# Attention scores masked by VectorE instead of TensorE, with the softmax division and one block load moved earlier

## The chip, the cores and the metric

The kernel runs on one core of one Trainium2 chip. The metric is the device time of one launch, in microseconds (us), on that core. TensorE multiplies matrices, VectorE and ScalarE work element by element on what it leaves in PSUM, GpSimd does the same on SBUF, and SyncE issues the transfers. [...]

## The reference

Three layers in a row. An attention over windows (32 heads in all, 768 positions, chunks of 32 queries that see 16 keys to the left, 8 to the right, and 8 memory keys), a dense layer with a gated activation, and a mixture of eight experts whose gates are balanced by eight rounds of normalisation.

```python
scores = scale * np.matmul(q_c, k_full.transpose(0, 1, 3, 2))
scores = scores - np.max(scores, axis=-1, keepdims=True)
a = np.exp(scores)
a = a / (np.sum(a, axis=-1, keepdims=True) + 1e-09)
out[:, :, c_start:c_end] = np.matmul(a, v_full)
...
h = x @ w_in
g = h * np.clip(h + 3.0, 0.0, 6.0) / 6.0
x = (g @ w_out)
...
for e in range(E):
    out += P[:, e:e + 1] * (np.maximum(x @ w1[e], 0.0) @ w2[e])
```

## The kernel before, in words

The program has three stages: a first stretch that holds the attention and the dense layer (two passes over the hidden columns of that layer), a short one for the gates, and the experts. The change lies in the first stretch alone.

**Attention units.** The attention is cut into 32 units of 96 queries (three chunks) by 128 keys, all eight heads of one batch entry. The three chunks of a unit see different keys, so a mask (0 or a very large negative number) has to be added to the scores. `a_scores` does that on TensorE: for each half of four heads, one product of two short bf16 tables (`mask`, L266) writes the mask into a PSUM bank (`sc`), and the four products of queries and keys (L272) add to it. Then, for a unit: `a_max` takes the row maxima of both halves on VectorE (`mx`, L279) and `a_neg` scales them (`nm`, L285); `a_exp` takes the exponentials on ScalarE, one instruction per head with its row sum (`e<-sc`, L297); `a_norm` divides on VectorE (`sm`, `rc`, `e<-e,rc`, L305 to L308); `a_transpose` turns the eight blocks on TensorE (`pt`, L315) and copies them out on ScalarE (`et`, L167); `a_values` multiplies by the values (`av`, L335); and `a_split` writes the result as a high part (ScalarE, `xh`, L167), a low part (VectorE, `xl`, L353) and their sum for later use (GpSimd, L359).

**The dense layer** runs in steps, numbered `i`: one step is one block of rows and one slice of 128 hidden columns. A step has a first product (`layer_product`, `ph`), an activation (`layer_relu` on ScalarE, L405; `layer_times` on VectorE, L410), a split into parts (`hh` on ScalarE, L167; `hl` on VectorE, L427), and, two steps later, a second product (`second`, `pa`). Every product is three products of float parts (L229 to L231). The first pass has 64 steps with blocks of 384 rows, the second 48 with blocks of 512.

**What sets the order.** Units 0 to 13 and the first 16 steps are issued by a list of words (`OPENING`). From step 17 on, a loop issues one unit per two steps. The odd step has, in program order, the first product and its activation and split, then values and split of unit u, scores and maximum of unit u+2, the second product, the exponentials of u+2, and the division of u+1. The even step has its first product and activation, the second product, the transposes of the unit, and only then its split:

```python
            if due:
                stage(a_values, u)
                stage(a_split, u)
                stage(a_scores, u + 2)
                stage(a_max, u + 2)
                ...
            second(i - LAG)
            ...
            if due:
                stage(a_exp, u + 2)
                stage(a_load, u + 4)
                stage(a_norm, u + 1)
```

In the same loop ScalarE and VectorE still convert weights (L147, L149; L158, L160), GpSimd combines expert weights (L692), and at the end of each block the accumulators are emptied: the second block's by VectorE (L500) in step 17, the later ones by ScalarE (L505). In the last block of the first pass `x_load(0)` fetches the first block of rows for the second pass in step f = 1 and `x_split(0, r)` splits it in steps f = 3 to 6.

Of the kernel before, what the change touches and what calls it, by code (L numbers as in the profile page):

```python
# [9 lines left out]
F32 = mybir.dt.float32  # L10
# [3 lines left out]
AF = mybir.ActivationFunctionType  # L14
ALU = mybir.AluOpType
AX = mybir.AxisListType
PSUM = bass.MemoryType.PSUM

D = 64
NH = 8  # L20
UQ = 96
UK = 128
# [4 lines left out]
UPS = 8  # L27
# [6 lines left out]
B2 = 512  # L34
# [6 lines left out]
LEAD = 1  # L41
STEADY = 12
EARLY = (1, 2, 3, 4, 5, 6, 7, 8, 9)
OPENING = (
# [22 lines left out]
def attn_moe_moe(ctx: ExitStack, tc: tile.TileContext, qk, vw, wi, wo, wa, wb, wg, out):  # L67
    nc = tc.nc
# [16 lines left out]
    sm_p = ctx.enter_context(pool("sm", 2))  # L85
    dr_p = ctx.enter_context(tc.tile_pool(name="dr", bufs=1, space=bass.MemoryType.DRAM))
    one, two, three = (ExitStack() for _ in range(3))
    ps_a = one.enter_context(pool("ps_a", 4, PSUM))
# [142 lines left out]
        nc.tensor.matmul(ps, wl, xh, start=False, stop=stop, skip_group_check=more)  # L231


    qk_t, v_t, sc_t, e_t, pt_t, et_t, av_t = {}, {}, {}, {}, {}, {}, {}
    xs = {}
    mask = []

# [7 lines left out]
    def mask_load(_):  # L245
# [5 lines left out]
        nc.vector.tensor_copy(out=mask[0][:3], in_=t[:3])  # L251
        nc.vector.tensor_copy(out=mask[0][D:D + 3], in_=mask[0][:3])

    def v_load(u):
        t = at_p.tile([UK, NH * D], F32, tag="vw", name="vw", bufs=2)
        nc.sync.dma_start(out=t, in_=vw[u])
        v_t[u] = t

    def a_scores(u):

        t, ps, tag = qk_t.pop(u), *((ps_a, "a") if u in EARLY else (ps_s, "s"))
        seen = {0: 0, UPS - 1: 1}.get(u % UPS, 2)
        for j in range(2):
            sc_t[u, j] = ps.tile([UQ, 4, UK], F32, tag=tag, name="sc")
            m = mask[0][D * j:D * j + D]
            nc.tensor.matmul(  # L266
                sc_t[u, j], m[:, 0, :UQ], m[:, seen, UQ:].unsqueeze(1).to_broadcast([D, 4, UK]),
                start=True, stop=False, skip_group_check=True)
        for i in range(4):
            for j in range(2):  # L270
                k = t[D * j:D * j + D, i]
                nc.tensor.matmul(  # L272
                    sc_t[u, j][:, i], k[:, :UQ], k[:, UQ:], start=False, stop=i == 3, skip_group_check=True)

    def a_max(u, halves=(0, 1)):
        for j in halves:
            if j == 0:
                e_t[u] = sm_p.tile([UQ, NH], F32, tag="mx", name="mx")
            nc.vector.tensor_reduce(out=e_t[u][:, 4 * j:4 * j + 4], in_=sc_t[u, j], axis=AX.X, op=ALU.max)  # L279
        if len(halves) == 2:  # L280
            a_neg(u)

    def a_neg(u):
        nm = sm_p.tile([UQ, NH], F32, tag="nm", name="nm")
        nc.vector.tensor_scalar_mul(nm, e_t[u], -SCALE)  # L285
        e_t[u] = nm

    def a_exp(u, halves=(0, 1)):
        for j in halves:
            if j == 0:  # L290
                ef = at_p.tile([UQ, NH, UK], F32, tag="e", name="e", bufs=2)
                sm = sm_p.tile([UQ, NH], F32, tag="sm", name="sm")
                e_t[u] = e_t[u], ef, sm
            nm, ef, sm = e_t[u]
            sc = sc_t.pop((u, j))
            for h in range(4 * j, 4 * j + 4):
                nc.scalar.activation(  # L297
                    out=ef[:, h], in_=sc[:, h % 4], func=AF.Exp, scale=SCALE, bias=nm[:, h:h + 1],
                    accum_out=sm[:, h:h + 1])
        if 1 in halves:  # L300
            e_t[u] = ef, sm
# [68 lines left out]
    def x_tiles():  # L370
        return [x_p.tile([128, KT, B1], F32R, tag=f"x{t}", name=f"x{t}") for t in "hl"]
# [7 lines left out]
    def stage(do, u):  # L379
        if u < NU:  # L380
            do(u)
# [81 lines left out]

    def opening(do, i):
        acts = {
            "qk": a_load, "mk": mask_load, "sc": a_scores, "v": v_load, "raw": raw_load, "sp": spill_one, "xps": spill_x2, "wg": gate_weights,
            "no": idle, "nm": a_neg, "n": a_norm, "V": a_values, "xh": a_high, "xl": a_low, "xf": a_whole,
            "ca": single_act, "cv": single, "hi": single_hi, "lo": single_lo,
            "F": layer_product, "re": layer_relu, "t": layer_times, "hh": layer_high, "hl": layer_low}
        two = {"mx": a_max, "ex": a_exp}  # L470
        if do in acts:
            acts[do](i)
        elif do[0] == "D":
            {"hi": single_hi, "xh": a_high, "hh": layer_high,
             "eta": lambda u, e: a_copy(u, 0, e), "etb": lambda u, e: a_copy(u, 1, e)}[do[1:]](i, nc.vector)
        elif do[:2] in two:
            two[do[:2]](i, (0,) if do[2] == "a" else (1,))
        elif do[0] == "T":
            a_turn(i, "ab".index(do[1]))
        elif do[:2] == "et":  # L480
            a_copy(i, "ab".index(do[2]))
        elif do == "S":
            second(i, False)
        elif do == "ev":
            evacuate(*steps[i])
# [32 lines left out]
    xq = []  # L518

    def x_pieces():  # L520
        return [t.rearrange("p k n -> p (k n)").rearrange("p (k n) -> p k n", n=B2) for t in x_tiles()]

    def x_load(b):
        if b < 2:
            xq.extend(x_pieces() for _ in range(2 - b))
        for kt in range(KT):
            n, at = ((0, kt) if kt < 3 else (1, 0)) if b % 2 == 0 else ((2, kt) if kt < 3 else (1, 1))
            xs.setdefault((1, b), []).append([t[:, at] for t in xq[n]])
        u = b * B2 // UQ
        t = xl_p.tile([128, UPB, KT, UQ], F32, tag="xl", name="xl")  # L530
        spare = [v[:, 2, :KT * UQ].bitcast(F32).rearrange("p (k q) -> p k q", k=KT) for v in xq[1]]
        c = UPB - u % UPB
        nc.sync.dma_start(out=t[:, :c], in_=xd[u // UPB][:, UPB - c:])
        if c < UPB:
            nc.sync.dma_start(out=t[:, c:], in_=xd[u // UPB + 1][:, :UPB - c])
        for i in range(2):
            v = u + UPB + i
            nc.sync.dma_start(out=spare[i], in_=xd[v // UPB][:, v % UPB])
        parts = []
        for i in range(UPB + 2):  # L540
            a, e = (min(max(v - b * B2, 0), B2) for v in (UQ * (u + i), UQ * (u + i + 1)))
            o = a + b * B2 - UQ * (u + i)
            whole = i < UPB and e - a == UQ
            if whole and parts and parts[-1][0] == "whole":
                parts[-1] = "whole", parts[-1][1], e, parts[-1][3], i + 1
            elif whole:
                parts.append(("whole", a, e, i, i + 1))
            else:
                parts.append(("part", a, e, t[:, i] if i < UPB else spare[i - UPB], o))
        xf_t[b] = t, parts  # L550
# [116 lines left out]
    w1s, w1, w2s, w2, gq, op, yc = {}, {}, {}, {}, {}, {}, {}  # L667
# [466 lines left out]
    with tc.manual_schedule():  # L1134
        at_ctx = pool("at", 2, side="right")
        at_p = at_ctx.__enter__()
# [3 lines left out]
        make_identity(nc, ident)  # L1140
        for word in OPENING:
            opening(word.rstrip("0123456789"), int(word.lstrip("abcdefghijklmnopqrstuvwxyzABCDEFGHIJKLMNOPQRSTUVWXYZ")))
# [19 lines left out]
        for i, (pe, b, f) in enumerate(steps):  # L1162
            if i < 2 * NF:
                continue
            u, turn, due = (i - 2 * NF) // 2 + 3 * UPB, i % 2 == 0, i % 2 == 1
# [22 lines left out]
            sums_due(i)  # L1188
            if pe == 0 and b == NB1 - 1:
                w_load(f)  # L1190
                if f == 1:
                    x_load(0)
            if pe == 1 and f == 1 and b + 1 < NB2:
                x_load(b + 1)
# [7 lines left out]
            if due:  # L1202
                stage(a_values, u)
                stage(a_split, u)
                stage(a_scores, u + 2)
                stage(a_max, u + 2)
                convert_act(rate(i))
                stage(v_load, u + 2)
# [8 lines left out]
            if due:  # L1217
                stage(a_exp, u + 2)
                stage(a_load, u + 4)
                stage(a_norm, u + 1)  # L1220
            if pe == 0 and not due:
                if turn:
                    stage(a_transpose, u)
# [7 lines left out]
                w_split(NF - LAG + f)  # L1231

            n = b + 1 if pe else 0
            r = f - 3
            if 0 <= r < KT and n < NB2 and (pe or b == NB1 - 1):
                x_split(n, r)
            if (pe, b, f) == (1, 2, 6):
# [44 lines left out]
        at = {o: i for i, (_, o) in enumerate(order)}  # L1282
        makes = {}
        for n in range(NM):
            for mi in range(7):
                for r in range(4):
                    i = at[n, mi - 1, r] if mi else at[n, 0, 0] - 4 + r
# [3 lines left out]
        halves, fours, quarter_work = {}, {}, None  # L1291
        sums = {}
        for sb in range(1, NSB):
# [5 lines left out]
            for r in range(2, 12):  # L1299
                i = base + (r + (r - 2) // 2 if sb == 1 else r + 7 if r > 2 else 8)  # L1300
# [11 lines left out]
        for i, (h, o) in enumerate(order):  # L1312
# [26 lines left out]
            if h and h[1] in FORM:  # L1339
                deep_out(*h, 0)  # L1340
                while lows:
                    do, n = lows.pop(0)
# [5 lines left out]
            while lows:  # L1348
                do, n = lows.pop(0)
# [9 lines left out]
            if h and h[1] in FORM:  # L1359
                n, _, p = h  # L1360
# [12 lines left out]
            elif h:  # L1373
                n, k, p = h
# [19 lines left out]
            if i in fours:  # L1394
                rows = []
                for q in range(2):
                    t = out_p.tile([128, HB], F32, tag="o", name="xs", bufs=NO)
# [71 lines left out]
```

## Time and profile before

| | before |
|---|---|
| median of 3 runs (lowest, highest) | 2497.66 us (2496.04, 2498.72) |
| profiled execution: its own time | 2497.8 us |
| its span, first to last instruction | 2496.0 us |
| TensorE busy | 2483.2 us (99%) |
| VectorE, ScalarE, GpSimd busy | 1967.8, 1443.9, 951.4 us |
| granted TensorE clock | 1.000 |

A busy share is the time in which an engine has an instruction in flight. In a timeline row stand start, length, engine, line, operation, output and inputs, the number of instructions joined in the row, and in brackets how long the engine stood idle before it and what it waited for. A start-to-start distance says more than a length here, since an instruction's end overlaps the next one's start.

### The profile page before, as it was taken

To read this page: it belongs to the slowest core of one execution; us is meant where nothing else is said; L and a number is where in the kernel's file an instruction comes from. 1 tells how busy PE (TensorE), PEld (TensorE's weight loads), DVE (VectorE), ACT (ScalarE), POOL (GpSimd) and SP (SyncE) were. 2 spreads that over 40 slices of the span, in tenths; PEclk is the share of its full clock that TensorE was granted. 3 is DMA by queue.
4 is the path that set the end of the run, shared out by engine and by line. 5 is a ranking of instruction groups with operands and counts; after the bars stand their busy time and mean duration, and the time that the engine had idled before them with its cause. 6 is when DMAs were issued, how large, how long until landed. Compare 5 with 4: busy or idle time off the path is not lost. (4 is left out here: it accounts for less than half of the span.)

```text
span 2496.0 us, 37061 instructions
## 1 busy us (share of the span) xinstructions
PE 2483.2 (99%) x13125; PEld 2123.1 (85%) x13125; DVE 1967.8 (79%) x2422; ACT 1443.9 (58%) x2685; POOL 951.4 (38%) x705
## 2 busy tenths in 40 slices
PE   9999999999999999999999999999999999999999
PEld 8999998787778888888888888888888888888888
DVE  8867656576689999999986778777888678777777
ACT  8666653222365565556666665656666666655665
POOL 0155656665025554533443324333323233132321
PEclk9999999999999999999999999999999999999999
DMA  7689988877466766766667777666777667676664
GB/s 210 188 279 312 302 271 294 292 269 256 135 214 208 228 214 229 226 221 226 232 233 253 262 257 246 221 214 232 251 267 237 223 223 229 227 231 213 213 220 155
DMA packets 379990, 587.45 MB, mean 235 GB/s; under 512 B 30675, under 2 KB 229276, under 8 KB 379804
## 3 DMA queue, kind: packets, MB, share of 16 engines
q1 hardware_dynamic: 379520, 584.85, 72.0%
q8 instruction: 103, 1.69, 0.3%
q14 instruction: 83, 0.68, 0.1%
q10 hardware_dynamic: 284, 0.24, 0.0%
HBM read 444.36 MB, written 140.61 MB: 234 GB/s over the span
## 5 line engine op out<-in xcount | busy, mean ns | idle before, releaser
L986 POOL TENSOR_TENSOR g<-g,pb 128x512 f32<-128x512 f32 x304 | 564.9, 1876 | 1181.4 <-ACT g L979 849.4
L1037 ACT ACTIVATE oh<-g 128x1024 fp32r<-128x1024 f32 x336 | 355.1, 1057 | 357.8 <-PE oa L231 107.2
L1042 DVE TENSOR_TENSOR ol<-g,oh 128x1024 fp32r<-128x1024 f32 x336 | 456.2, 1359 | 56.4 <-ACT oh L1037 56.1
L692 POOL TENSOR_TENSOR fr<-fr 128x256 f32<-128x256 f32 x320 | 278.1, 870 | 180.0 <-DMA fr<-in_wa_dram 88.2
L229 PE MATMUL ga<-xo,w1h 128*128 128x512 f32 (+1 forms) x864 | 314.1, 364 | 2.1 <-ACT g L954 1.5
L230 PE MATMUL ga<-xo,w1h 128*128 128x512 f32 (+1 forms) x864 | 312.5, 362 | 0.0
L231 PE MATMUL ga<-xo,w1l 128*128 128x512 f32 (+1 forms) x864 | 312.5, 362 | 0.0
L1012 DVE TENSOR_TENSOR g<-g 128x1024 f32<-128x1024 f32 x192 | 302.0, 1611 | 0.0
L230 PE MATMUL oa<-ol,w2h 128*128 128x512 f32 x760 | 298.0, 392 | 0.0
L229 PE MATMUL oa<-oh,w2h 128*128 128x512 f32 x760 | 297.5, 391 | 0.0
L231 PE MATMUL oa<-oh,w2l 128*128 128x512 f32 x760 | 296.1, 390 | 0.0
L859 ACT ACTIVATE w1h<-w1s 128x512 fp32r<-128x512 f32 (+1 forms) x416 | 249.9, 601 | 39.3 <-issue 19.0
L971 DVE TENSOR_TENSOR g<-g,ga 128x512 f32<-128x512 f32 x192 | 130.4, 679 | 103.7 <-PE ga L231 103.5
L405 ACT ACTIVATE t<-ph,half 128x384 f32<-128x384 f32 (+1 forms) x112 | 70.5, 630 | 242.1 <-PE ph L231 236.9
L979 ACT ACTIVATE g<-g 128x512 f32<-128x512 f32 x288 | 178.0, 619 | 40.5 <-DVE g L971 40.3
L229 PE MATMUL gc<-xo,w1h 128*128 128x512 f32 (+1 forms) x544 | 195.6, 359 | 1.6 <-ACT g L954 0.8
L896 ACT ACTIVATE w2h<-w2s 128x1024 fp32r<-128x1024 f32 x168 | 176.9, 1053 | 32.0 <-DMA w2s<-in_wb_dram 21.2
L231 PE MATMUL gc<-xo,w1l 128*128 128x512 f32 (+1 forms) x544 | 194.7, 358 | 0.0
L230 PE MATMUL gc<-xo,w1h 128*128 128x512 f32 (+1 forms) x544 | 194.6, 358 | 0.0
L229 PEld LDWEIGHTS ga<-xo,w1h 128*128 128x128 f32 x864 | 162.6, 188 | 35.4 <-ACT g L954 3.4
L230 PEld LDWEIGHTS ga<-xo,w1h 128*128 128x128 f32 x864 | 162.6, 188 | 28.5
L231 PEld LDWEIGHTS ga<-xo,w1l 128*128 128x128 f32 x864 | 162.5, 188 | 25.0
(188 smaller groups left out, 5657.6 us busy)
## 6 DMA issues: line engine op xcount, KB each, us to landing
w1l<-wl SPq DMA_DIRECT2D x232, 256.0 KB, 4.2
w2l<-wl SPq DMA_DIRECT2D x112, 512.0 KB, 3.8
w1s<-ws SPq DMA_DIRECT2D x192, 256.0 KB, 4.9
w2s<-ws SPq DMA_DIRECT2D x96, 512.0 KB, 4.9
ws<-fr SPq DMA_DIRECT2D x80, 512.0 KB, 5.0
w2s<-in_wb_dram SPq DMA_DIRECT2D x144, 256.0 KB, 3.6
wl<-w1l SPq DMA_DIRECT2D x128, 256.0 KB, 4.0
wl<-w2l SPq DMA_DIRECT2D x56, 512.0 KB, 4.4
```

The costliest lines, as they stand in the source:

```text
L229: nc.tensor.matmul(ps, wh, xh, start=start, stop=False, skip_group_check=more)
L230: nc.tensor.matmul(ps, wh, xl, start=False, stop=False, skip_group_check=more)
L231: nc.tensor.matmul(ps, wl, xh, start=False, stop=stop, skip_group_check=more)
L692: nc.gpsimd.tensor_tensor(out=o, in0=a, in1=b, op=f)
L859: nc.scalar.activation(out=w1_part(g, w1[g]), in_=w1_part(g, w1s[g]), func=AF.Copy)
L896: nc.scalar.activation(out=hi, in_=w2s[m], func=AF.Copy)
L971: nc.vector.tensor_tensor(out=g, in0=g, in1=ps, op=ALU.add)
L979: nc.scalar.activation(out=g, in_=g, func=AF.Relu)
L986: nc.gpsimd.tensor_tensor(out=g, in0=g, in1=p, op=ALU.mult)
L1012: nc.vector.tensor_tensor(out=o, in0=gq[n, x, i], in1=gq[n, y, i], op=ALU.subtract)
L1037: nc.scalar.activation(out=hi, in_=gq[n, b, i], func=AF.Copy)
L1042: nc.vector.tensor_tensor(out=lo, in0=gq[n, b, i], in1=op[m, i].bitcast(F32), op=ALU.subtract)
```

## The change

- From unit 14 on (all units of the loop) the mask is no longer a product. Ahead of the first unit, `mask_make` forms the three masks in PSUM by three small products and ScalarE copies them once into SBUF (`mk`). `a_max` then adds the mask to each half of the scores on VectorE, writing to the SBUF tile `e`, takes the maxima of all eight heads by one reduction of that tile, and `a_exp` reads `e` instead of PSUM.
- In the odd step the division of unit u+1 stands right behind the split of unit u, ahead of scores and maximum of u+2. Before, it stood at the end of the step.
- `x_load(0)` is issued in step f = 0 of the last block instead of f = 1, `x_split(0, r)` in f = 2 to 5 instead of 3 to 6, and the two pieces of memory that the block uses change places.

```diff
+ADDED = 14
 OPENING = (
-    "mk0 qk0 no12 sc0 mxa0 raw3 ...
+    "mk0 qk0 no12 mm0 sc0 mxa0 raw3 ...
...
+    def mask_make(_):
+        m = mask[0][:D]
+        ps = ps_a.tile([UQ, 3, UK], F32, tag="a", name="sc")
+        for k in range(3):
+            nc.tensor.matmul(ps[:, k], m[:, 0, :UQ], m[:, k, UQ:], start=k == 0, stop=k == 2, skip_group_check=True)
+        t = sm_p.tile([128, B2], F32, tag="lt", name="mk", bufs=1)[:UQ, :3 * UK]
+        mask.append(t.rearrange("p (k n) -> p k n", k=3))
+        nc.scalar.activation(out=mask[1], in_=ps, func=AF.Copy)
...
     def a_scores(u):
...
-            nc.tensor.matmul(
-                sc_t[u, j], m[:, 0, :UQ], m[:, seen, UQ:].unsqueeze(1).to_broadcast([D, 4, UK]),
-                start=True, stop=False, skip_group_check=True)
+            if u < ADDED:
+                nc.tensor.matmul(
+                    sc_t[u, j], m[:, 0, :UQ], m[:, kind(u), UQ:].unsqueeze(1).to_broadcast([D, 4, UK]),
+                    start=True, stop=False, skip_group_check=True)
...
     def a_max(u, halves=(0, 1)):
         for j in halves:
             if j == 0:
                 e_t[u] = sm_p.tile([UQ, NH], F32, tag="mx", name="mx")
-            nc.vector.tensor_reduce(out=e_t[u][:, 4 * j:4 * j + 4], in_=sc_t[u, j], axis=AX.X, op=ALU.max)
+                if u >= ADDED:
+                    ef_t[u] = at_p.tile([UQ, NH, UK], F32, tag="e", name="e", bufs=2)
+            if u >= ADDED:
+                nc.vector.tensor_tensor(
+                    out=ef_t[u][:, 4 * j:4 * j + 4], in0=sc_t.pop((u, j)),
+                    in1=mask[1][:, kind(u)].unsqueeze(1).to_broadcast([UQ, 4, UK]), op=ALU.add)
...
         if len(halves) == 2:
+            if u >= ADDED:
+                nc.vector.tensor_reduce(out=e_t[u], in_=ef_t[u], axis=AX.X, op=ALU.max)
             a_neg(u)
...
     def a_exp(u, halves=(0, 1)):
...
-            sc = sc_t.pop((u, j))
+            sc = ef[:, 4 * j:4 * j + 4] if u >= ADDED else sc_t.pop((u, j))
...
-            xq.extend(x_pieces() for _ in range(2 - b))
+            xq.extend([x_pieces() for _ in range(2 - b)][::-1])
...
-                if f == 1:
+                if f == 0:
                     x_load(0)
...
                 stage(a_split, u)
+                stage(a_norm, u + 1)
                 stage(a_scores, u + 2)
...
                 stage(a_load, u + 4)
-                stage(a_norm, u + 1)
...
-            r = f - 3
+            r = f - 2 - pe
```

How the instructions of one unit stand on VectorE in the middle of the loop, before (`hl` and `t` belong to the dense layer, `sa` and `sb` to the conversion of weights, the rest is named above):

```order
L427 TENSOR_TENSOR hl<-t,hh 128x384
L353 TENSOR_TENSOR xl<-av,xh 128x4x96
L279 TENSOR_REDUCE mx<-sc 96x4 x2
L285 TENSOR_SCALAR nm<-mx 96x8
L305 TENSOR_SCALAR sm<-sm 96x8
L307 RECIPROCAL rc<-sm 96x8
L308 TENSOR_TENSOR e<-e,rc 96x1024
L158 SCALAR_TENSOR_TENSOR sa<-raw,rest 128x512
L160 SCALAR_TENSOR_TENSOR sa<-pw,sa 128x512
L410 SCALAR_TENSOR_TENSOR t<-t,ph 128x384
```

And the same unit on VectorE in the changed kernel:

```order
L452 TENSOR_TENSOR hl<-t,hh 128x384
L378 TENSOR_TENSOR xl<-av,xh 128x4x96
L330 TENSOR_SCALAR sm<-sm 96x8
L332 RECIPROCAL rc<-sm 96x8
L333 TENSOR_TENSOR e<-e,rc 96x1024
L297 TENSOR_TENSOR e<-sc,mk 96x512 x2
L305 TENSOR_REDUCE mx<-e 96x8
L310 TENSOR_SCALAR nm<-mx 96x8
L159 SCALAR_TENSOR_TENSOR sa<-raw,rest 128x512
L161 SCALAR_TENSOR_TENSOR sa<-pw,sa 128x512
L435 SCALAR_TENSOR_TENSOR t<-t,ph 128x384
```

Between `xl` and `nm` there stood two instructions before; now there stand six, the three of the division among them.

ScalarE in the changed kernel, over the same stretch of the loop (L430 is the activation of a step, L168 the copies `et`, `hh` and `xh`, L322 the exponentials):

```order
L322 ACTIVATE e,sm<-e,nm 96x128 x8
L430 ACTIVATE t<-ph,half 128x384
L168 ACTIVATE et<-pt 128x384 x2
L168 ACTIVATE hh<-t 128x384
L430 ACTIVATE t<-ph,half 128x384
L168 ACTIVATE hh<-t 128x384
L168 ACTIVATE xh<-av 128x4x96
L148 ACTIVATE rest<-raw 128x512
```

Here nothing moved; only the exponentials read `e` where they read `sc` before. The copies `et`, which the values product of the next unit needs, stand behind the eight exponentials.

## Rows read from the trace of the kernel before

**Rows 1.** Windows, loop and after: length; PE, PEld, DVE, ACT, POOL busy; clock, DMA.

```profile
137.00:332.00 195.00, 194.76 (x1554) 184.40 (x1556) 132.84 (x222) 128.45 (x441) 113.56 (x125) 1.00 0.99 307
300.00:660.00 360.00, 360.00 (x1819) 304.85 (x1818) 225.14 (x365) 113.02 (x285) 198.08 (x228) 1.00 0.78 258
```

**Rows 2.** Timeline of PE, one unit of the loop.

```profile
162.71 0.88 PE L335 MATMUL av<-et,vw 128*64 128x96 f32 x16
163.52 0.42 PE L266 MATMUL sc<-mask 64*96 64x512 bf16 x2
163.77 1.04 PE L272 MATMUL sc<-qk 64*96 64x128 f32 x16
...
173.98 0.88 PE L335 MATMUL av<-et,vw 128*64 128x96 f32 x16
```

**Rows 3.** Timeline of ACT, the same unit.

```profile
162.88 0.58 ACT L405 ACTIVATE t<-ph,half 128x384 f32<-128x384 f32 x1 [1.23 <-PE ph L231]
164.07 0.52 ACT L167 ACTIVATE hh<-t 128x384 fp32r<-128x384 f32 x1 [0.62 <-DVE t L410]
164.50 0.47 ACT L167 ACTIVATE xh<-av 128x384 fp32r<-128x384 f32 x1
...
167.14 0.36 ACT L297 ACTIVATE e<-sc,nm 96x128 f32<-96x128 f32 x1 [1.06 <-DVE sm L305]
...
169.90 0.60 ACT L405 ACTIVATE t<-ph,half 128x384 f32<-128x384 f32 x1
171.64 0.87 ACT L167 ACTIVATE et<-pt 128x384 f32<-128x384 f32 x2 [1.15 <-PE pt L315]
172.40 0.53 ACT L167 ACTIVATE hh<-t 128x384 fp32r<-128x384 f32 x1
```

**Rows 4.** Timeline of DVE, the same unit.

```profile
164.63 0.56 DVE L427 TENSOR_TENSOR hl<-t,hh 128x384 fp32r<-128x384 f32 x1 [0.59 <-ACT hh L167]
165.10 0.55 DVE L353 TENSOR_TENSOR xl<-av,xh 128x384 fp32r<-128x384 f32 x1
165.57 1.27 DVE L279 TENSOR_REDUCE mx<-sc 96x4 f32<-96x512 f32 x2
166.88 0.17 DVE L285 TENSOR_SCALAR nm<-mx 96x8 f32<-96x8 f32 x1
166.96 0.16 DVE L305 TENSOR_SCALAR sm<-sm 96x8 f32<-96x8 f32 x1
...
168.53 1.23 DVE L158 SCALAR_TENSOR_TENSOR sa<-raw,rest 128x512 uint32<-128x512 uint32 x1
```

**Rows 5.** Groups by form, 137 to 332 us: count, busy, mean ns, idle before.

```profile
L427 DVE TENSOR_TENSOR hl<-t,hh 128x384 fp32r<-128x384 f32 x35 | 25.6, 730 | 33.6 <-ACT hh L167 33.6
L279 DVE TENSOR_REDUCE mx<-sc 96x4 f32<-96x512 f32 x34 | 21.6, 676 | 0.0
L285 DVE TENSOR_SCALAR nm<-mx 96x8 f32<-96x8 f32 x17 | 5.3, 309 | 0.6
L167 ACT ACTIVATE hh<-t 128x384 fp32r<-128x384 f32 x35 | 18.4, 525 | 10.9 <-DVE t L410 10.9
L167 ACT ACTIVATE et<-pt 128x384 f32<-128x384 f32 x36 | 15.7, 489 | 14.7 <-PE pt L315 14.7
```

**Rows 6.** One line, a reduction out of SBUF: ns least, median, most.

```profile
L605 DVE TENSOR_REDUCE rs<-Pm x8: 352/353/354, 660.4 to 692.0; 128x24 f32<-128x192 f32 x8
```

**Rows 7.** Timelines of DVE and PE around step 17.

```profile
130.80 0.54 DVE L353 TENSOR_TENSOR xl<-av,xh 128x384 fp32r<-128x384 f32 x1
133.07 1.93 DVE L500 TENSOR_TENSOR x<-x,pa 128x384 f32<-128x384 f32 x4
134.19 0.33 PE L229 MATMUL pa<-hh,wbh 128*128 128x384 f32 x1
137.24 0.85 PE L315 MATMUL pt<-ident,e 96*128 96x96 f32 x8 [0.81 <-DVE e L308]
```

**Rows 8.** Timeline of ACT in the opening: its first work.

```profile
7.51 0.66 ACT L147 ACTIVATE rest<-raw 128x512 uint32<-128x512 uint32 x1 [4.25 <-DMA raw<-in_wi_dram]
```

More of the change, by code (lines that the diff above doesn't have):

```diff
@@ L231, in passes @@
         nc.tensor.matmul(ps, wl, xh, start=False, stop=stop, skip_group_check=more)
-    qk_t, v_t, sc_t, e_t, pt_t, et_t, av_t = {}, {}, {}, {}, {}, {}, {}
+    qk_t, v_t, sc_t, e_t, pt_t, et_t, av_t, ef_t = {}, {}, {}, {}, {}, {}, {}, {}
     xs = {}
@@ L252, in mask_load, with kind @@
         nc.vector.tensor_copy(out=mask[0][D:D + 3], in_=mask[0][:3])
+    def mask_make(_):
[6 more added lines that the diff above has]
+        nc.scalar.activation(out=mask[1], in_=ps, func=AF.Copy)
+    def kind(u):
+        return {0: 0, UPS - 1: 1}.get(u % UPS, 2)
     def v_load(u):
@@ L261, in a_scores @@
         t, ps, tag = qk_t.pop(u), *((ps_a, "a") if u in EARLY else (ps_s, "s"))
-        seen = {0: 0, UPS - 1: 1}.get(u % UPS, 2)
         for j in range(2):
@@ L272, in a_scores @@
                 nc.tensor.matmul(
-                    sc_t[u, j][:, i], k[:, :UQ], k[:, UQ:], start=False, stop=i == 3, skip_group_check=True)
+                    sc_t[u, j][:, i], k[:, :UQ], k[:, UQ:], start=u >= ADDED and i == 0, stop=i == 3,
+                    skip_group_check=True)
     def a_max(u, halves=(0, 1)):
@@ L278, in a_max @@
                 e_t[u] = sm_p.tile([UQ, NH], F32, tag="mx", name="mx")
-            nc.vector.tensor_reduce(out=e_t[u][:, 4 * j:4 * j + 4], in_=sc_t[u, j], axis=AX.X, op=ALU.max)
+                if u >= ADDED:
[4 more added lines that the diff above has]
+                    in1=mask[1][:, kind(u)].unsqueeze(1).to_broadcast([UQ, 4, UK]), op=ALU.add)
+            if u < ADDED or len(halves) == 1:
+                at = sc_t[u, j] if u < ADDED else ef_t[u][:, 4 * j:4 * j + 4]
+                nc.vector.tensor_reduce(out=e_t[u][:, 4 * j:4 * j + 4], in_=at, axis=AX.X, op=ALU.max)
         if len(halves) == 2:
+            if u >= ADDED:
+                nc.vector.tensor_reduce(out=e_t[u], in_=ef_t[u], axis=AX.X, op=ALU.max)
             a_neg(u)
@@ L290, in a_exp @@
             if j == 0:
-                ef = at_p.tile([UQ, NH, UK], F32, tag="e", name="e", bufs=2)
+                ef = ef_t.pop(u) if u >= ADDED else at_p.tile([UQ, NH, UK], F32, tag="e", name="e", bufs=2)
                 sm = sm_p.tile([UQ, NH], F32, tag="sm", name="sm")
@@ L465, in opening @@
         acts = {
-            "qk": a_load, "mk": mask_load, "sc": a_scores, "v": v_load, "raw": raw_load, "sp": spill_one, "xps": spill_x2, "wg": gate_weights,
+            "qk": a_load, "mk": mask_load, "mm": mask_make, "sc": a_scores, "v": v_load, "raw": raw_load, "sp": spill_one, "xps": spill_x2, "wg": gate_weights,
             "no": idle, "nm": a_neg, "n": a_norm, "V": a_values, "xh": a_high, "xl": a_low, "xf": a_whole,
```

2 rows, old and new, of the table OPENING are left out of this document.

## The prediction

> **What bounds the kernel now.** I read the busy shares by stretch first, then the timelines of the three engines that an attention unit passes through, and last the lengths of single kinds of instruction. The windows are to show whether anything but TensorE can set the time: from 137 to 332 us, where the loop runs, TensorE is busy 194.76 of 195 us, and from 300 to 660 us it has no gap at all [rows 1]. So in the kernel before, only what TensorE executes counts. TensorE's timeline gives the length of one unit (two steps): values product to values product, 173.98 - 162.71 = 11.27 us, of which the mask holds 163.77 - 163.52 = 0.25 us [rows 2]. Its two products are recorded with 0.42 us, but the queries' products start 0.25 us behind them, and that is what removing them gives.
>
> The question is then what the others need. The timelines of ScalarE and VectorE [rows 3, 4] show a ring that closes from unit to unit without TensorE: ScalarE's copies `et` of one unit, then `hh`, the activation and `hh` of the next step, `xh`; VectorE's `hl` and `xl`; the maximum and `nm`; ScalarE's exponentials; the even step's activation; and the next `et`. Each stands in the queue behind the one before, or waits for it. Before the change the legs of this ring are, by start-to-start distances:
>
> - end of `et` to start of `xl`, when ScalarE never waits for TensorE: `hh` starts 0.11 us before the end of the pair `et` (172.40 against 172.51), the next instruction 0.43 us behind an `hh` (164.50 - 164.07), and from that activation to `xl` 165.10 - 162.88 = 2.22 us; together 2.54.
> - `xl` to `nm`: 166.88 - 165.10 = 1.78.
> - `nm` to the even step's activation: 0.26 to the first exponential, 2.76 for eight; 3.02.
> - activation to end of `et`: 0.60 less 0.09 of overlap, and 0.87; 1.38.
>
> The sum is 8.72 us of 11.27, a slack of 2.55. The trace confirms it in another way: `et` waits 1.15 us for the transposes, and from its end, 172.51, to the values product at 173.98 there are 1.47 us more, 2.62 together [rows 2, 3]. **The change has to be paid out of these 2.6 us, 18 times.**
>
> **The change part by part.** The sum is made against the profiled execution's own 2497.8 us, 0.1 us over the median of the runs.
>
> *Mask off TensorE:* 18 units (14 to 31), 0.25 us each, -4.5 us on TensorE [rows 2]; its work for one unit becomes 11.02 us.
>
> *Mask on VectorE, division in front of the maximum:* both lengthen the same leg, `xl` to `nm`. It becomes 0.47 (`xl` to the next start) + 1.57 (the division, from `sm` at 166.96 to the next start at 168.53) + 1.31 (two additions of 512 columns out of PSUM, taken like the two reductions of 512 columns, 165.57 to 166.88) [rows 4] + the reduction of 1024 columns. One of 192 columns out of SBUF takes 353 ns [rows 6], one of 512 out of PSUM 676 [rows 5], 1.01 ns per column; 1024 then take 1.19 us, and 0.04 for the result to arrive: 1.23. The leg is 4.58 instead of 1.78, so the ring grows by 2.80 us, more than its slack. Bare, it is 2.54 + 4.58 + 3.02 + 1.38 = 11.52.
>
> *Exponentials out of SBUF:* the trace has none. Its nearest rows are two copies of 384 columns on ScalarE, 489 ns out of PSUM (`et`) and 525 out of SBUF (`hh`) [rows 5]: 0.036 us each, 0.29 for eight. [...] Ring: 11.81.
>
> [...]
>
> *Delays inside the ring:* `hl` takes 0.56 us in the row of one unit [rows 4] and 0.73 on average, `nm` 0.17 and 0.31 [rows 4, 5]. While there is slack this costs nothing; in a ring without slack each counts. One `hl` and one `nm`: 0.17 + 0.14 = 0.31. The ends are 0 and twice that, 0.62, when the other `hl` and `sm`, which now follows `xl` as `nm` follows the maximum, are stretched likewise. I take 0.31, what the trace has. Ring: 12.12 us, and TensorE with its 11.02 us of work waits at the values product for `et`, 1.1 us in every unit.
>
> *Step 17* is a case of its own, since VectorE empties an accumulator there. Behind `xl` at 130.80 now come 0.47 + 1.57 + 1.31 + 1.23 + 0.08 us before it starts on that, at 135.46 instead of 133.07, and the first quarter is out 0.55 later, at 136.0. TensorE wants that bank at 134.19 - 0.25 = 133.94 and waits 2.06 us. In return its wait of 0.81 us for the division [rows 7] goes, as the division is done by 132.9. Net of the mask: +1.0 us.
>
> *`mask_make`:* ScalarE's copy lies in the 4.25 us in which it waits for its first data [rows 8]; the three short products delay the first scores by no more than the 0.25 us of a mask. I take 0; ends 0 and +0.2.
>
> *`x_load` and `x_split` a step sooner:* TensorE has no gap from 300 to 660 us [rows 1], so nothing is to be won. The three transfers pass two weight loads, a spill and a store and load of GpSimd's work in SyncE's queue; those loads are used two steps later. 0. Everything behind the first pass only shifts.
>
> Sum: 17 units by 12.12 - 11.27 = 0.85 are 14.5, and 1.0 for step 17: **+15.5 us, 2513.3 us.** With both unknowns at their low ends (11.52) it is 17 x 0.25 + 1.0 = +5.3, 2503.1; at the high ends (12.43, and the opening's 0.2) +20.9, 2518.7.
>
> **The rivals.**
>
> *TensorE stays the bound (faster).* If the new ring came to 11.02 us or less, TensorE would never wait for it, and the change would give -4.5 - 0.8 + 2.1 = -3.2 us: 2494.6. It decides at the wait of the values product for `et`. For it: VectorE and ScalarE are busy only 133 and 128 of 195 us [rows 1]. Against it: that is an average, and the legs added from rows without any stretch already give 11.52. It needs a division or a reduction half a microsecond shorter than these rows.
>
> *The ring just fits (no difference).* Between 11.02 and 11.5 us the saved mask and the new waits cancel: 2495 to 2503, about 2500. It needs exponentials no dearer, no stretched instruction, and a little off the reduction.
>
> *The ring is longer still (slower by more).* GpSimd is busy 113.56 of 195 us [rows 1], and if the stretched `hl` and `nm` come from that, the division and both `hl` may be held as well. With 1.0 us of such delays the ring is 12.81: 17 x 1.54 + 1.0 = +27.2, 2525. [...]
>
> That the change doesn't do what it says is no rival: the order shows the additions and the early division in all 18 units.
>
> **How the numbers follow.** A measurement of this kernel tells 0.2%, 5.0 us, from no change. The forecast (ring between 11.5 and 12.5 us) has 0.74, since its sum is bare rows and its unknowns only add; the longer ring 0.07; the ring that just fits 0.11; TensorE as the bound 0.08. Slower is 0.74 + 0.07 = 0.81, no difference 0.11, faster 0.08. The range runs from 2500, which takes in the bounds below and the upper part of the ring that just fits, to 2520; left out are the two outer cases and some of the third, not quite 0.2.
>
> **What would show it.** Right: TensorE's waits in the loop, nearly none before, come to about 1 us per unit, at `av` and on ScalarE's `et`, and one of 2 us at `pa` in step 17, on VectorE's L500 (its new number aside); units about 12.1 us apart; ScalarE going from the exponentials to the activation to `et` without a pause; `xl` to `nm` about 4.6 us; exponentials about 0.4 us long. Wrong: units 11.0 us apart with `et` finished before TensorE comes to it; or `nm` less than 4 us behind `xl`; or a new wait elsewhere, such as at the head of the second pass.

## The result and the profile after

| | before | after |
|---|---|---|
| median of 5 runs, us (lowest, highest) | 2497.62 (2496.04, 2498.72) | 2522.18 (2520.29, 2523.14) |
| ratio, with its 95% interval | | 1.0099 [1.0084, 1.0113] |
| span of the profiled execution, us | 2496.0 | 2519.9 |

The change makes the kernel slower by 24.6 us, 1.0%. The forecast was slower by 15.5 us, 2513.3, and its range ended at 2520: the direction is right, the size is not.

The kernel after still looks bound by TensorE on the page (busy time, share of the span, instructions):

```profile
PE 2484.1 (99%) x13092; PEld 2125.0 (84%) x13092; DVE 1995.3 (79%) x2440; ACT 1445.8 (57%) x2686; POOL 947.5 (38%) x705
```

The stretch of the units tells another story. First the window over it, with the columns of [rows 1]; then, from the timeline of PE, the values products of the units that open step 17, that follow it, and that end the stretch:

```profile
143.00:356.00 213.00, 193.28 (x1500) 182.86 (x1498) 150.55 (x234) 128.38 (x436) 113.14 (x125) 0.99 0.89 278
```

```profile
127.94 0.88 PE L360 MATMUL av<-et,vw 128*64 128x96 f32 x16
...
143.59 0.88 PE L360 MATMUL av<-et,vw 128*64 128x96 f32 x16
...
356.25 0.99 PE L360 MATMUL av<-et,vw 128*64 128x96 f32 x16 [1.51 <-ACT et L168]
```

TensorE now stands idle 19.7 of 213 us, where before it had 0.24 of 195 [rows 1]. Before, the same three values products stood here:

```profile
127.87 0.88 PE L335 MATMUL av<-et,vw 128*64 128x96 f32 x16
...
140.16 0.88 PE L335 MATMUL av<-et,vw 128*64 128x96 f32 x16
...
331.81 0.88 PE L335 MATMUL av<-et,vw 128*64 128x96 f32 x16
```

Step 17's unit has grown from 12.29 to 15.65 us, 3.36 more; the 17 units behind it from 191.65 to 212.66, which is 12.51 instead of 11.27 for one, 21.0 more together. That is 24.4 us, all there is: up to the first of these rows the change costs 0.07 us, and from the last to the end the kernel takes 2163.7 us against 2164.2. What TensorE waits for (the waits of PE over the whole kernel: total, times, longest, in us):

```profile
PE av L360 <- ACT et L168: 20.5, 18, 2.0
PE pa L230 <- DVE x L525: 2.8, 1, 2.8
```

The waits are where the forecast put them, the values product on ScalarE's `et` and, once, `pa` on VectorE's emptying of the accumulator. Why a unit takes 12.5 us on average shows in two that follow each other. From the timeline of DVE, from one `xl` to the next `nm`, twice (the conversions and the dense layer between them left out):

```profile
171.35 0.55 DVE L378 TENSOR_TENSOR xl<-av,xh 128x384 fp32r<-128x384 f32 x1
...
172.24 1.22 DVE L333 TENSOR_TENSOR e<-e,rc 96x1024 f32<-96x1024 f32 x1
173.38 1.28 DVE L297 TENSOR_TENSOR e<-sc,mk 96x512 f32<-96x512 f32 x2
174.69 1.22 DVE L305 TENSOR_REDUCE mx<-e 96x8 f32<-96x1024 f32 x1
175.95 0.58 DVE L310 TENSOR_SCALAR nm<-mx 96x8 f32<-96x8 f32 x1
...
183.51 0.55 DVE L378 TENSOR_TENSOR xl<-av,xh 128x384 fp32r<-128x384 f32 x1
...
184.40 1.85 DVE L333 TENSOR_TENSOR e<-e,rc 96x1024 f32<-96x1024 f32 x1
186.18 1.27 DVE L297 TENSOR_TENSOR e<-sc,mk 96x512 f32<-96x512 f32 x2
...
188.73 0.59 DVE L310 TENSOR_SCALAR nm<-mx 96x8 f32<-96x8 f32 x1
```

and GpSimd's work in the same two units, from the timeline of POOL (`fr` is its combination of expert weights, `xf` its sum of `xh` and `xl`):

```profile
173.15 3.35 POOL L717 TENSOR_TENSOR fr<-fr 128x256 f32<-128x256 f32 x4 [7.58 <-DMA fr<-in_wb_dram]
176.46 1.54 POOL L384 TENSOR_TENSOR xf<-xh,xl 128x384 f32<-128x384 f32 x1
...
184.14 1.03 POOL L384 TENSOR_TENSOR xf<-xh,xl 128x384 f32<-128x384 f32 x1 [2.57 <-DVE sm L330]
```

In the first unit `xl` is done at 171.9 us, but in GpSimd's queue the four `fr` stand ahead of `xf`, and they wait for a transfer until 173.15; `xf` comes at 176.46, and the division takes 1.22 us. In the second nothing stands ahead of `xf`: it and the division both follow the end of `xl`, `xf` 0.26 us ahead, and the division takes 1.85. What a kind of instruction can take, from the answer on the tile `e` on DVE, 143 to 356 us (ns: least, median, most):

```profile
L297 DVE TENSOR_TENSOR e<-sc,mk x34: 671/675/683, 148.2 to 349.3; 96x512 f32<-96x512 f32 x34
L333 DVE TENSOR_TENSOR e<-e,rc x17: 1220/1836/1848, 146.9 to 347.0; 96x1024 f32<-96x1024 f32 x17
L305 DVE TENSOR_REDUCE mx<-e x17: 1215/1216/1218, 149.5 to 350.0; 96x8 f32<-96x1024 f32 x17
```

The additions and the reduction never vary by more than 12 ns. The division is held by about 0.62 us in 9 of 17 units, each time beside `xf`; by 0.2 and 0.4 in two, beside `fr`; and it is free in 6. `nm`, 0.17 us when alone, is held too; in the groups by form of the same stretch (as [rows 5]) it averages 518 ns, and the exponentials out of SBUF stand with 389 (365 out of PSUM before):

```profile
L310 DVE TENSOR_SCALAR nm<-mx 96x8 f32<-96x8 f32 x17 | 8.8, 518 | 0.6
L322 ACT ACTIVATE e<-e,nm 96x128 f32<-96x128 f32 x136 | 52.7, 389 | 71.3 <-DVE nm L310 71.3
```

What holds `nm` can be read beside it. In the first of the two units above it takes 0.58 us from 175.95 on, and this is in flight on POOL:

```profile
175.77 0.73 POOL L717 TENSOR_TENSOR fr<-fr 128x256 f32<-128x256 f32 x1
```

In 14 of the 17 units a GpSimd instruction is in flight like that when `nm` starts, 13 times an `fr` and once `xf`, and `nm` ends 0.02 to 0.03 us behind it. In the other three none is in flight then for more than 0.05 us longer, and it takes 0.17 us.

Step 17 is the other part. Its rows on DVE and then on PE, which answer to [rows 7]:

```profile
131.66 1.76 DVE L333 TENSOR_TENSOR e<-e,rc 96x1024 f32<-96x1024 f32 x1
...
135.90 0.54 DVE L310 TENSOR_SCALAR nm<-mx 96x8 f32<-96x8 f32 x1
136.36 1.93 DVE L525 TENSOR_TENSOR x<-x,pa 128x384 f32<-128x384 f32 x4
```

```profile
137.04 0.66 PE L230 MATMUL pa<-hh,wbh 128*128 128x384 f32 x1 [2.80 <-DVE x L525]
137.50 0.52 PE L231 MATMUL pa<-hl,wbh 128*128 128x384 f32 x1
137.82 0.52 PE L232 MATMUL pa<-hh,wbl 128*128 128x384 f32 x1
...
140.72 0.82 PE L340 MATMUL pt<-ident,e 96*128 96x96 f32 x8
```

`pa` waits 2.80 us, and behind that wait its products start 0.32 us apart instead of 0.17 us. The granted clock tells why (windows of 2 us; columns of [rows 1], the clock third from the end):

```profile
134.00:136.00 2.00, 0.24 (x2) 0.00 (x0) 1.93 (x4) 0.00 (x0) 1.76 (x4) 1.00 0.00 0
...
138.00:140.00 2.00, 2.00 (x8) 2.00 (x7) 1.58 (x3) 2.00 (x11) 0.00 (x0) 0.50 0.12 23
...
278.00:280.00 2.00, 0.15 (x1) 0.00 (x0) 0.52 (x1) 2.00 (x9) 0.00 (x0) 1.00 0.72 276
280.00:282.00 2.00, 1.86 (x18) 1.67 (x20) 1.06 (x3) 1.38 (x4) 0.00 (x0) 0.57 1.10 351
282.00:284.00 2.00, 2.00 (x18) 1.72 (x17) 1.68 (x5) 1.72 (x4) 0.00 (x0) 0.57 1.06 387
```

After the wait the clock is 0.50, and from 142 us on it is 1.00 again. It falls once more, to 0.57, behind the longest wait for `et`, 1.99 us up to 280.14.

### The profile page after: what moved, and what is told of

It is laid out like the page before. It is cut to its first block, busy times and chain, and to the rows that moved or that the text cites. A ratio compares the mean times of both kernels' runs of the same rounds, so it can differ in the third digit from the quotient of the medians.

```text
span 2519.9 us, 37015 instructions
## 1 busy us (share of the span) xinstructions
PE 2484.1 (99%) x13092; PEld 2125.0 (84%) x13092; DVE 1995.3 (79%) x2440; ACT 1445.8 (57%) x2686; POOL 947.5 (38%) x705
## 5 line engine op out<-in xcount | busy, mean ns | idle before, releaser
L430 ACT ACTIVATE t<-ph,half 128x384 f32<-128x384 f32 (+1 forms) x112 | 69.7, 622 | 219.5 <-PE ph L232 213.3
```

## The experiments

The first theory, the **ring**, is the prediction's: the queues of VectorE and ScalarE close from unit to unit, and every us put on that path is paid for once the path is longer than TensorE's work. Its sharper form after the result: the division stands in the ring, and where it stands now GpSimd's `xf` starts with it, and the division takes 1.84 to 1.85 us beside it instead of 1.22. That it does so because of GpSimd's instruction is the **port** theory of some expectations and the division theory of experiment 2. The rivals: **load** (the mask, with its exponentials out of SBUF, costs the time wherever the division stands) and **clock** (the waits cost little, the lowered clock much). All runs below were timed beside the kernel before, which took 2497.4 to 2497.5 us there.

**1. The division back behind the exponentials.** Mask and block load stay as changed.

```diff
                 stage(a_split, u)
-                stage(a_norm, u + 1)
                 stage(a_scores, u + 2)
...
                 stage(a_load, u + 4)
+                stage(a_norm, u + 1)
```

> The changed kernel with the division of unit u+1 back at the end of the odd step. Ring theory (the division and the mask addition both stand between xl and nm in a ring of VectorE and ScalarE queues that is longer than TensorE's work on a unit): without the 1.57 to 2.2 us of the division the ring is 2.54 + 3.05 + 0.3 to 0.6 + 3.10 + 1.30 = 10.3 to 10.6 us, under TensorE's 11.02. Units 11.02 us apart, no wait of the values product for et, about 2493 to 2495 us, a little faster than before. Load theory (VectorE's extra work costs time wherever the division stands): units stay over 11.5 us, above 2505 us. Clock theory (the loss comes from the granted clock of TensorE falling after the 2.8 us wait in step 17): that wait shrinks to under 1 us and the clock stays at 1.00, so this also predicts about 2494; it is told apart by the run with half of the units.

Measured: 2495.31 us, ratio 0.9991 [0.9982, 1.0000]; the ring theory had 2493 to 2495. This is the load theory's fall: the same work, on the same engines, costs nothing when the division stands behind `nm`. The timeline of PE shows units of 11.08 to 11.09 us, and among the waits of PE none for `et` is left in the loop; in a few units the transposes wait for a late division (`pt`, 6 times and 2.4 us in the whole kernel), and two units of the loop take 11.8 us:

```profile
184.43 0.88 PE L360 MATMUL av<-et,vw 128*64 128x96 f32 x16
...
195.52 0.88 PE L360 MATMUL av<-et,vw 128*64 128x96 f32 x16
```

So taking the mask off TensorE gives 11.27 - 11.08 = 0.19 us per unit, not the 0.25 that the start-to-start distance in [rows 2] promised. This is the one version that is not slower than the kernel before; its gain of 2 us can hardly be told from nothing.

**2. The mask back on TensorE,** the division and the block load as changed.

```diff
-ADDED = 14
+ADDED = 32
```

> The changed kernel with the mask left on TensorE for all units: only the division's place and the earlier block load are changed. Ring theory: ring 8.72 + 1.57 + 0.3 to 0.6 = 10.6 to 10.9 us, under TensorE's 11.27, so units stay 11.27 us apart and the time is 2496 to 2499 us; in step 17 the wait of 0.81 us for the division goes and one of 1.0 to 1.6 us for the emptied accumulator comes. Division theory (the division's new place is at fault by itself, as it meets GpSimd's addition xf there): slower by 5 to 20 us.

Measured: 2511.74 us, 1.0053 [1.0040, 1.0065]. The ring theory of the expectation missed by 13 us, and the division theory's 5 to 20 us came true: the division's new place alone costs 14 us, without any of the mask's work. But the meeting with `xf` is not all of it. The waits of PE, and one unit in the timelines of PE and DVE:

```profile
PE pt L340 <- ACT e L322: 9.2, 14, 0.8
```

```profile
184.99 0.55 PE L340 MATMUL pt<-ident,e 96*128 96x96 f32 x4 [0.65 <-ACT e L322]
...
187.61 0.88 PE L360 MATMUL av<-et,vw 128*64 128x96 f32 x16
...
199.19 0.88 PE L360 MATMUL av<-et,vw 128*64 128x96 f32 x16
```

```profile
190.01 0.55 DVE L378 TENSOR_TENSOR xl<-av,xh 128x384 fp32r<-128x384 f32 x1
...
193.36 0.20 DVE L310 TENSOR_SCALAR nm<-mx 96x8 f32<-96x8 f32 x1
```

This is a second ring, through TensorE. Scores and transposes share two PSUM banks. When the exponentials read their scores out of those banks, the transposes can't begin on one before its exponentials are done; behind the transposes stand the next first product (`ph`, to 187.6), the activation that waits for it (187.78), `xl` (190.01), `nm` (193.36, 3.35 later with the division in between), and the next exponentials, done at 196.5. From the transposes at 184.99 that is 11.5 us, more than the 11.27 of the kernel before, although the division takes its 1.22 us here. Units in which nothing is held take 11.57 us, the others 12.0 and more; the mean is 12.07. So of 0.80 us per unit 0.30 are the bare ring, 5 us in 17 units, and 0.50 are delays in it, 8.5 us, most of them divisions of 1.6 to 1.84 us. In the kernel before the division was not in it, 1.57 less, so it had slack. In the changed kernel the additions copy the scores out to SBUF, the banks come free early, and among the waits of PE there is none of `pt` for ScalarE's `e`, where here there are 9.2 us of it; only the ring through `et` remains. The sharing stands in the kernel (`sc` and `pt` come from one pool of two buffers, `ps_s`); that it closes the ring is read from the wait and from what the additions do to it, and a kernel with another bank was not tried.

**3. The division in the even step,** behind that step's `hl`, with the mask on VectorE.

```diff
                 stage(a_split, u)
-                stage(a_norm, u + 1)
...
                 first_parts(i)
+                stage(a_norm, u + 1)
```

> The changed kernel with the division of unit u+1 at the end of the even step, behind that step's hl, where VectorE stood idle before. Ring theory: the division is no part of xl to nm; it lies in the 1 to 2 us in which VectorE waits for the next step's activation. Ring 10.3 to 10.6 us, or up to 0.5 us more where the division pushes the next step's activation; units 11.02 us. In step 17 about 0.5 us of wait for the accumulator and none for the division. 2492 to 2494 us. Load theory: above 2505 us.

Measured: 2511.74 us, 1.0051 [1.0038, 1.0064]. Missed by 18 us, because the place was taken for one outside of the ring and isn't. The timeline of DVE:

```profile
187.07 0.56 DVE L452 TENSOR_TENSOR hl<-t,hh 128x384 fp32r<-128x384 f32 x1 [0.60 <-ACT hh L168]
...
187.98 1.22 DVE L333 TENSOR_TENSOR e<-e,rc 96x1024 f32<-96x1024 f32 x1
```

This `hl` follows `hh`, which stands behind `et` in ScalarE's queue, so the division moved from one leg of the ring to the one before: end of `et` to `xl` is 4.11 us instead of 2.54, `xl` to `nm` 3.03 instead of 4.60. The sum is unchanged. But the division is now free of `xf` (1.22 us in nearly all units), and the unit takes 12.01 us on average, not 12.51.

**4. The mask on VectorE for the later half of these units.**

```diff
-ADDED = 14
+ADDED = 23
```

> The changed kernel with the mask moved to VectorE only from unit 23 on (9 of the 18 units); the division in its new place for all. Ring theory: units 14 to 22 are 11.27 us, units 23 to 31 about 12.5 us as in the changed kernel; +11.2 us and up to +1 for step 17, 2507 to 2511 us. Clock theory: step 17 has no long wait, so nearly all of the loss goes, below 2501 us.

Measured: 2514.32 us, 1.0062 [1.0047, 1.0078]. Over the ring theory's number by 3 us, since that took the earlier units to be as short as before, and units 14 to 22 run at 12.0 us on average, as in experiment 2. The later ones take 12.2 to 13.2. The granted clock is 1.00 throughout and the kernel is still 17 us slower, so the clock is not the main cost: that rival falls.

**5. GpSimd's weight combination left out,** so that only `xf` remains of its work in the loop.

```diff
             def make():
-                for *v, f in ops:
-                    o, a, b = (piece(t[0], i) for i in v)
-                    nc.gpsimd.tensor_tensor(out=o, in0=a, in1=b, op=f)
+                pass
```

> The changed kernel without GpSimd's combination of expert weights (the loads and stores of that work stay, its arithmetic is left out), so that GpSimd's only work in the loop is the sum xf of each unit, which starts when xl ends. Port theory (VectorE's division and nm are stretched while GpSimd reads SBUF): nm is never held, so nm to the first exponential is 0.2 to 0.3 us in every unit instead of 0.55 on average; xf meets the division in every unit, so xl to nm is 5.2 us in all of them; units 2.54 + 5.22 + 0.2 + 3.10 + 1.30 = 12.36 us. Rival (the stretch comes from transfers or from ScalarE, not from GpSimd): units stay a mixture of 12.2 and 12.8 us.

Measured, in one execution: 2519.59 us. With less work on GpSimd the units get hardly shorter (12.39 us on average, not 12.51); but for the first, 12.16, they become all alike, 12.40 to 12.42. From the timelines of POOL and DVE:

```profile
183.58 1.02 POOL L384 TENSOR_TENSOR xf<-xh,xl 128x384 f32<-128x384 f32 x1 [11.38 <-DVE sm L330]
```

```profile
183.79 1.89 DVE L333 TENSOR_TENSOR e<-e,rc 96x1024 f32<-96x1024 f32 x1
...
188.17 0.17 DVE L310 TENSOR_SCALAR nm<-mx 96x8 f32<-96x8 f32 x1
```

GpSimd always waits for `xl` now, so `xf` meets the division in every unit, and the division takes 1.89 us on average over 17 units, most 1.90; `nm` is free in every unit, 168 ns on average. The one is what `xf` does, the other was the weight combination's doing. By what the one engine's instruction stretches the other's, no run shows. The rival, that transfers or ScalarE stretch them, had the units stay a mixture.

**6. The same, with the division ahead of the split,** so that `xf` can start only when the division is done.

```diff
                 stage(a_values, u)
-                stage(a_split, u)
                 stage(a_norm, u + 1)
+                stage(a_split, u)
```

> As the run before (GpSimd's combination of expert weights left out), with the division of unit u+1 ahead of the split of unit u instead of behind it, so that xf no longer meets it. Port theory: nothing is stretched; the division still lies in the ring, so units are 2.54 + 1.57 + 3.03 + 0.2 + 3.10 + 1.30 = 11.74 us, all alike. If the ring were not what sets the pace, units would be 11.1 us, as in the run with the division back at the end of the step.

Measured, in one execution: 2505.75 us, units 11.71 to 11.76 (the first 11.55). The timelines of DVE, POOL and PE:

```profile
190.63 1.22 DVE L333 TENSOR_TENSOR e<-e,rc 96x1024 f32<-96x1024 f32 x1
...
192.24 1.28 DVE L297 TENSOR_TENSOR e<-sc,mk 96x512 f32<-96x512 f32 x2
```

```profile
192.45 1.02 POOL L384 TENSOR_TENSOR xf<-xh,xl 128x384 f32<-128x384 f32 x1 [10.71 <-DVE xl L378]
```

```profile
187.62 0.98 PE L360 MATMUL av<-et,vw 128*64 128x96 f32 x16 [0.48 <-ACT et L168]
...
199.35 0.98 PE L360 MATMUL av<-et,vw 128*64 128x96 f32 x16 [0.48 <-ACT et L168]
```

`xf` now meets the additions, and neither is stretched: the two take 1.28 us, as in the changed kernel without `xf` beside them (1.27 to 1.28), and `xf` 1.02. In experiment 5 `xf`, 0.2 us ahead of the division, kept its 1.02 us as well, while the division got 0.67 longer. Why the division is held beside `xf` and the additions are not, no run shows. The unit is the sum of the ring's legs without any delay: 4.10 + 3.03 + 0.20 + 3.10 + 1.30 = 11.73.

**7. The division ahead of the split,** with GpSimd's work in place (the diff of experiment 6 alone).

> The changed kernel with the division of unit u+1 ahead of the split of unit u, all of GpSimd's work in place. Ring and port theory: the division stays in the ring but no longer starts with xf; units between 11.74 (nothing held) and 12.5 us, about 12.1 on average as in the run with the division in the even step; about 2512 us, against 2522 for the changed kernel.

Measured: 2512.52 us, 1.0058 [1.0043, 1.0073]; units 12.03 on average. As expected: 9.7 us of the 24.6 go when the division no longer meets `xf`; an `nm`, an `hl` or a division is still held now and then, the divisions beside `fr`.

**8. Unit 14's mask on TensorE,** the unit whose scores are taken in step 17.

```diff
-ADDED = 14
+ADDED = 15
```

> The changed kernel with unit 14, whose scores come in step 17, left with the mask on TensorE. Then the accumulator in step 17 is emptied about 1.2 us sooner. Clock theory for step 17 (its 15.65 us are 2.8 us of wait and a granted clock of half for some microseconds after it): the wait shrinks to 0.5 to 1.6 us, the clock stays at 1.00, and the unit takes 12.1 to 12.8 us; 2 to 3.5 us off the time, about 2519.5 us, with the other units unchanged. If the clock falls without a long wait, the unit stays over 14 us.

Measured: 2518.90 us, 1.0084 [1.0067, 1.0101]. Without the additions and the long reduction, VectorE comes to the accumulator in step 17 2.0 us sooner. From the timeline of PE, with the clock at 1.00 in the 6 us from 134 on:

```profile
135.03 0.41 PE L230 MATMUL pa<-hh,wbh 128*128 128x384 f32 x1 [0.71 <-DVE x L525]
...
137.19 0.82 PE L340 MATMUL pt<-ident,e 96*128 96x96 f32 x8
```

That step's unit takes 12.23 us instead of 15.65, the others are as before this edit, 12.5. From the first `pa` to the transposes it is 2.16 us here and 3.68 in the changed kernel, for the same 12 products: the lowered clock cost 1.5 us.

## Why the prediction was right in direction and wrong in size

**What bounds it: right.** The ring of the prediction is the cause. Its bare legs, taken from a kernel in which it was hidden, came out within 0.08 us: end of `et` to `xl` 2.54 (forecast 2.54), `xl` to `nm` 4.60 with a free division (4.58), activation to the end of `et` 1.30 (1.38). Experiment 6 shows the whole ring without delays at 11.73; the forecast had 11.81.

**Exponentials out of SBUF: right.** From the first exponential to the activation it is 3.10 us, against 2.75 before and 3.05 forecast, 0.35 more for eight, 44 ns each. The copies, from which I took 36, were 8 ns too low for each. That the exponentials cost no more out of SBUF, as the forecast's low end of 11.52 has it, no run shows: the 0.35 is there in every unit, 3.09 to 3.11 us.

**"Delays inside the ring": the step that failed most.** I took 0.31 us, one `hl` and one `nm`. Measured: 0.78. Over the 16 units behind the first the legs exceed the bare ones by 0.06 (`et` to `xl`), 0.38 (`xl` to `nm`) and 0.34 (`nm` to the first exponential, 0.54 instead of 0.20): 0.78, and 11.74 + 0.78 = 12.52, the length of a unit. Against the 12.12 of the forecast, 17 units of 12.51 are 6.6 of the 9.1 us by which it was short. The fault is not in the average but in where it was taken: the delays of the trace before belonged to the old order. In its new place the division follows the same event as `xf`, and I looked for who waits behind the division, not for what else starts with it. `hl`, which I did charge, became shorter (580 ns on average, 730 in [rows 5]). The sum's upper end, 0.62, was not high enough either; the rival that named the division as held ("the ring is longer still") had 1.0 us and 0.07 of the chance, and its 2525 is nearer to the result than my forecast. That is in part luck: its ring of 12.81 was 0.3 us too long, and its step 17 was 2.4 us too short.

**Step 17: mechanism right, price wrong.** The forecast was a wait of 2.06 us, less 0.81 and 0.25, +1.0. Measured +3.36. The wait is 2.80, since the division took 1.76 us and `nm` 0.54 there; and 1.5 us more come from the lowered clock after the wait, which the sum had nowhere. In experiment 8, where the wait is 0.71 us, the clock stays up and the step's unit takes 12.23 us.

**Mask off TensorE: right in kind, 0.19 us instead of 0.25** (experiment 1). In the changed kernel it buys nothing, since TensorE waits.

**`mask_make`, `x_load`, `x_split`: right, 0.** 0.07 us in the opening, and nothing lost behind the loop.

**The rivals.** That TensorE stays the bound, or that the ring just fits, is excluded by 18 waits for `et`. What no rival held: that the new place of the division by itself costs 14 us (experiment 2), by a ring through the score banks and by the delays in it. My argument treated mask and division as two lengths added to one path; in fact the additions also relieve the second path, so the parts don't add: mask alone about nothing (-2 us), division alone +14, both +25.

**Left open:** whether the ring of experiment 2 goes when scores and transposes get banks of their own, and how often `xf` meets the division under another order of GpSimd's queue.

## What to carry to other kernels

Before putting an instruction earlier in a queue, follow the path that returns from unit to unit through the queues of all engines, and sum its legs: an engine that is busy 71% (VectorE, 150.55 of 213 us) can still be the bound, and work the ring doesn't need belongs behind the ring's last instruction on that engine (here `nm`), not in front. Then ask what another engine starts on the same event: two instructions that are released together can meet unit after unit (in experiment 5 in every one), while the averages of the old trace tell of the meetings in the old order. And a change that frees a buffer earlier and one that uses it later are not to be priced apart; run each alone.

## What was unexpected of the hardware

TensorE's granted clock fell behind a single wait in an otherwise busy stretch: to 0.50 (138 to 140 us) after 2.80 us of waiting, to 0.57 over the 4 us after 1.99 us. In experiment 7 it was 0.50 again, from 138 to 140 us, behind the wait of 1.96 us at `pa`, and in experiment 5, where `pa` waits 2.1 us, 0.93 over the 20 us from 120 on. In the changed kernel the waits of 0.7 to 1.6 us in the other units were followed by 1.00, and so were the longest ones in experiments 4 and 8, 1.87 and 1.81 us. The first fall cost 1.5 us on top of the wait.

Engines met here without waiting for each other: an instruction of VectorE took longer beside one of GpSimd that it did not depend on, the division 1.84 to 1.85 us beside `xf` instead of 1.22. Even one of 96 x 8 elements, `nm`, takes 0.17 us alone and in the changed kernel up to 0.67 beside an `fr` and 0.74 beside `xf`, nearly as much added as the division of 96 x 1024 gets from `xf`.
